# One DMA transpose for two units of dS in an attention backward loop

## The chip, the cores and the metric

The kernel runs on one core of a Trainium2 chip. The metric is the device time of one execution in microseconds, lower being better; every execution is timed on the device, and the median of several is taken.

## What is computed

The reference is the forward and backward pass of one transformer block (batch 1, 2048 tokens, width 512): layer norm with modulation by a conditioning vector, attention with 32 heads of 16 channels, and a feed-forward layer with a squared ReLU. The kernel returns the block's output and nine gradients. The part that matters here is the backward pass of attention:

```python
qkv = (x @ wqkv).reshape(B, S, 3, H, Dh)              # H = 32, Dh = 16
scores = einsum('bhqd,bhkd->bhqk', q, k) * Dh ** -0.5
p = softmax(scores, axis=-1)
o = einsum('bhqk,bhkd->bhqd', p, v)
...
_out, _vjp = jax.vjp(_f, A_x, A_wqkv, A_wo, B_w1, B_b1, B_w2, B_b2, c, w_mod)
_grads = _vjp(grad_out)
```

For every head it needs dS = p * (dP - delta), where dP = dO V^T, and from it dK = dS^T Q and dQ = dS K. The products for dK and dV contract over queries, and dS as it is computed (queries on the partitions) serves them directly. The product for dQ contracts over keys, so dS is needed a second time with keys on the partitions. That second form is made by a DMA transpose.

## The kernel before

The forward pass, the feed-forward backward pass and the gradients of the weights stand before and after the loop in question. The backward attention loop (lines 748 to 909) runs over **units**. A unit is one group of four heads (`hg`, 8 of them), one chunk of 512 keys (`kc`, 4), and one tile of 128 queries; the queries are counted as four tiles (`qi`) in each of four chunks (`qc`). There are 8 x 4 x 4 x 4 = 512 units, and four units that differ only in `qi` form a **block**; there are 128 blocks. Each unit is worked on in two half-units (`j`, two heads each).

For each unit:

- `score` (L791): TensorE multiplies Q and K for one head into PSUM (`psS_u`, or `psS_x`, which shares a bank with `dqacc`), and ScalarE takes the exponential into `E_u`.
- `dp_pair` (L807): TensorE makes dP for two heads in `psD_u` (two buffers), and VectorE multiplies it with `E_u` into `dS_u` (128 queries x 4 heads x 512 keys, bf16, 512 KB). The row maximum and delta are subtracted inside the matmuls, through extra rows of the operands.
- `transpose_unit` (L819): SyncE issues one DMA transpose of the unit's `dS_u` into one quarter of `dsT`, the block's tile.
- `k_quad` and `v_quad` (L825, L834): two units later TensorE accumulates dK from `dS_u` and dV from `E_u` in `accVK`.
- `dq_quad` (L850): in the last two half-units of the *next* block, TensorE multiplies the keys with the block's four transposed tiles into `dqacc`; ScalarE scales the result into `dQacc` or `dqtmp`, and GpSimd adds it up.

The order of the instructions on TensorE, ScalarE, VectorE and SyncE is the order in which this loop writes them (`manual_schedule`, L888); each engine runs its own in that order, and semaphores make it wait for the others. A half-unit issues its two scores, the dP pair of the half-unit before it, the transpose (if a unit was just completed), a k or v quad of two units earlier, and, at `sub` 6 and 7, the dq quads:

```python
                b = j // 8 - 1
                if sub >= 6 and 0 <= b < NU // 4:
                    for kt in (2 * (sub - 6), 2 * (sub - 6) + 1):
                        dq_quad(b, kt)
```

So between a block's last transpose (issued at j = 8b + 8) and its first dq quad (j = 8b + 14) lie six half-units of other work. `E_u` and `dS_u` have four buffers each (pool `ework`), `dsT` has two. Loads for the next group of heads are issued by ScalarE (`load`, L776) at planned half-units; the SyncE queue carries the transposes and, in the last group, four loads of gradients (`load_grads`, L742). After the loop another scheduler orders the remaining instructions.

Of the kernel before, what the change touches and what calls it, by code (L numbers as in the profile page):

```python
# [17 lines left out]
BF = dt.bfloat16  # L18
F32 = dt.float32

P = 128
# [13 lines left out]
def kernel(  # L35
# [21 lines left out]
    SP = nc.sync  # L57
# [221 lines left out]
    with ExitStack() as ph:  # L279
        wk = ph.enter_context(tc.tile_pool(name="phC", bufs=2))  # L280
        ework = ph.enter_context(tc.tile_pool(name="phCe", bufs=4))
# [364 lines left out]
        with ExitStack() as ph2:  # L646
# [3 lines left out]
            with tc.manual_schedule(engines={PE.engine, ACT.engine}):  # L650
                for u in range(NF + 6):
# [18 lines left out]
                    if pend and pend[0][0] <= u and not open_group[0] and not stepped:  # L670
                        _, f, args = pend.pop(0)
# [26 lines left out]
        with ExitStack() as ph2:  # L698
            pools["mm"] = ph2.enter_context(tc.tile_pool(name="psM2", bufs=8, space=bass.MemoryType.PSUM))
            while dense:  # L700
                for _ in dense.pop(0):
                    clock[0] += 1
                    if pend and not open_group[0] and pend[0][0] + 2 <= clock[0]:
                        _, f, args = pend.pop(0)
# [43 lines left out]
    with ExitStack() as ph:  # L748
        ework = ph.enter_context(tc.tile_pool(name="phIe", bufs=4))
# [7 lines left out]
        hst, bst, dqt, cur = {}, {}, {}, {}  # L757
# [12 lines left out]
        def at(j, f, *args):  # L770
            todo.setdefault(j, []).append((f, args))
# [19 lines left out]
        def score(u, hq, shared):  # L791
            hg, kc, qc, qi = units[u]
            st = hst[hg]
            qt = qc * 4 + qi
            if hq == 0:
                bst[u] = (ework.tile([P, 4, 512], BF, name="E_u", tag="E_u"),
                          ework.tile([P, 4, 512], BF, name="dS_u", tag="dS_u"))
            r = 32 * hq
            if shared:
                psS = psx.tile([P, 512], F32, name="psS_x", tag="px")  # L800
            else:
                psS = pss.tile([P, 512], F32, name="psS_u", tag="ps")
            PE.matmul(psS[:], st["q"][r:r + 32, qt * P:(qt + 1) * P], st["k"][r:r + 32, kc * 512:kc * 512 + 512],  # L803
                      start=True, stop=True, tile_position=(r, 0))
            ACT.activation(bst[u][0][:, hq, :], psS[:], AF.Exp, scale=SCALE)  # L805

        def dp_pair(u, pair):  # L807
            hg, kc, qc, qi = units[u]
            st = hst[hg]
            qt = qc * 4 + qi  # L810
            E_u, dS_u = bst[u]
            psD = psd.tile([P, 2, 512], F32, name="psD_u", tag="pd")
            for hi in range(2):
                r = 32 * (2 * pair + hi)
                PE.matmul(psD[:, hi, :], st["do"][r:r + 32, qt * P:(qt + 1) * P], st["v"][r:r + 32, kc * 512:kc * 512 + 512],  # L815
                          start=True, stop=True, tile_position=(r, 0))
            DVE.tensor_tensor(dS_u[:, 2 * pair:2 * pair + 2, :], psD[:], E_u[:, 2 * pair:2 * pair + 2, :], ALU.mult)  # L817

        def transpose_unit(u):  # L819
            hg, kc, qc, qi = units[u]  # L820
            if qi == 0:
                dqt[u // 4] = tpool.tile([P, 4, 16, P], BF, name="dsT", tag="dsT")
            SP.dma_start(out=dqt[u // 4][:, qi], in_=bst[u][1].rearrange("p h k -> p (h k)"), transpose=True)

        def k_quad(u):  # L825
            hg, kc, qc, qi = units[u]
# [7 lines left out]
        def v_quad(u):  # L834
            hg, kc, qc, qi = units[u]
            qt = qc * 4 + qi
            E_u, dS_u = bst.pop(u)
            acc = cur["vk"]
            for hq in range(4):
                PE.matmul(acc[32 * hq:32 * hq + DH, :], dOs_tok[:, qt, (hg * 4 + hq) * DH:(hg * 4 + hq + 1) * DH], E_u[:, hq, :],  # L840
                          start=False, stop=(qt == TT - 1), tile_position=(0, 32 * hq), skip_group_check=True)
            if qt == TT - 1:
                ACT.activation(hst[hg]["vk"][:, kc * 512:(kc + 1) * 512], acc[:], AF.Identity)  # L843
                if kc == QC - 1:
                    if hg >= HG - 2:
                        xs[hg, "vk"] = hst[hg]["vk"]
                    else:
                        at(cur["j"] + 4, load, dVKtP[hg], hst[hg]["vk"][:])
# [39 lines left out]
        with tc.manual_schedule(engines={PE.engine, ACT.engine, DVE.engine, SP.engine}):  # L888
            for j in range(2 * NU + 10):
                u, pair, sub = j // 2, j % 2, j % 8  # L890
                cur["j"] = j
                if j < 2 * NU:
                    if pair == 0 and units[u][1:] == (0, 2, 0) and units[u][0] + 1 < HG:
                        load_head(units[u][0] + 1)
                    for hi in range(2):
                        score(u, 2 * pair + hi, sub < 6 and (2 * sub + hi) % 3 == 2)
                if 1 <= j <= 2 * NU:
                    dp_pair((j - 1) // 2, (j - 1) % 2)
                    if (j - 1) % 2 == 1:
                        transpose_unit((j - 1) // 2)  # L900
                if 2 <= u < NU + 2:
                    (k_quad if pair == 0 else v_quad)(u - 2)
# [4 lines that stand above are left out]
                for f, args in todo.pop(j, ()):  # L907
                    f(*args)
            assert not todo
# [234 lines left out]
```

## Time and profile before

| | before |
|---|---|
| device time, median of 3 runs | 3060.49 us (3059.92 to 3061.36) |
| the profiled execution's own time | 3064.67 us |
| its span (first to last instruction) | 3062.8 us |
| the loop: first to last dS multiplication on VectorE | 1436.8 to 2872.4 us of the span |
| busy over the span: TensorE / ScalarE / VectorE / GpSimd | 81% / 71% / 58% / 17% |
| mean granted TensorE clock | 0.806 |
| DMA transposes of dS | 512, of 512 KB each |

The profile is one execution of the kernel. Its page gives busy shares of each engine, the span in 40 slices, the chain of work that ended last, and the costliest groups of instructions with the idle time before them and what ended it. PE is TensorE, PEld its weight loads, DVE VectorE, ACT ScalarE, POOL GpSimd, SP SyncE; a "q" behind the name (SPq) is the engine's sequencer, which issues DMAs. L823 is line 823 of the kernel. The busy time of SPq on a DMA is the time of issuing; the data move later, and a DMA piece in the chain runs from the issue to the landing.

### The profile page before, as it was taken

To read this page: it belongs to the slowest core of one execution; us is meant where nothing else is said; L and a number is where in the kernel's file an instruction comes from. 1 tells how busy PE (TensorE), PEld (TensorE's weight loads), DVE (VectorE), ACT (ScalarE), POOL (GpSimd) and SP (SyncE) were. 2 spreads that over 40 slices of the span, in tenths; PEclk is the share of its full clock that TensorE was granted. 3 is DMA by queue.
4 is the path that set the end of the run, shared out by engine and by line. 5 is a ranking of instruction groups with operands and counts; after the bars stand their busy time and mean duration, and the time that the engine had idled before them with its cause. 6 is when DMAs were issued, how large, how long until landed. Compare 5 with 4: busy or idle time off the path is not lost.

```text
span 3062.8 us, 46283 instructions
## 1 busy us (share of the span) xinstructions
PE 2481.7 (81%) x17006; PEld 720.8 (24%) x17006; DVE 1786.0 (58%) x2165; ACT 2181.0 (71%) x3415; POOL 519.5 (17%) x487
## 2 busy tenths in 40 slices
PE   6789888688867885565888888989888988888878
PEld 2111122222212221221222222222222222222323
DVE  6000134333513351446888878878887888878783
ACT  4699989698958894201777877878777877877521
POOL 2110012220332033313010110101011010101151
PEclk9555579878976997687888888878887798878889
DMA  9750142633394439596999999999999999999931
GB/s 258 189 134 18 30 74 82 150 92 81 81 162 65 95 79 151 103 165 189 205 200 208 199 202 199 197 206 202 208 197 201 201 198 205 204 204 204 212 107 52
DMA packets 1403811, 475.54 MB, mean 155 GB/s; under 512 B 1321456, under 2 KB 1372660, under 8 KB 1403456
## 3 DMA queue, kind: packets, MB, share of 16 engines
q1 hardware_dynamic: 1384624, 431.18, 73.8%
q0 software_dynamic: 12384, 25.17, 5.0%
q10 hardware_dynamic: 6576, 16.23, 1.6%
q8 instruction: 134, 2.20, 0.3%
q14 instruction: 93, 0.76, 0.1%
HBM read 74.86 MB, written 70.54 MB: 47 GB/s over the span
## 4 chain that ended last, share of the span: by engine, by line
PE 24%; DMA 19%; ACT 5%; DVE 5%; issue 3%; POOL 1%; SPq 1%; ACTq 0%; DVEq 0%; POOLq 0%
DMA dsT<-dS_u 16%; PE psS_u L803 7%; PE dqacc L858 5%; ACT E_u L805 5%; PE accVK L840 3%; PE accVK L831 3%; PE psS_x L803 2%; DVE dS_u L817 2%; DMA dwp<-dw_st 2%; PE pwq L1060 1%; PE psD_u L815 1%; SPq L954 0%; DMA out_dram<-dwm 0%; ACT vkb L843 0%; PE pm L496 0%
## 5 line engine op out<-in xcount | busy, mean ns | idle before, releaser
L817 DVE TENSOR_TENSOR dS_u<-psD_u,E_u 128x1024 bf16<-128x1024 f32 x1024 | 1190.4, 1218 | 250.0 <-PE psD_u L815 155.3
L573 ACT ACTIVATE ET<-psST 128x1024 bf16<-128x1024 f32 x1024 | 952.1, 1224 | 169.8 <-PE psST L571 168.8
L805 ACT ACTIVATE E_u<-psS_u 128x512 bf16<-128x512 f32 x1536 | 866.1, 632 | 272.0 <-PE psD_u L815 258.7
L805 ACT ACTIVATE E_u<-psS_x 128x512 bf16<-128x512 f32 x512 | 331.8, 648 | 18.0 <-PE psD_u L815 12.7
L858 PE MATMUL dqacc<-dsT,KS_tok 128*32 128x512 bf16 x2048 | 214.4, 506 | 140.8 <-DMA dsT<-dS_u 116.8
L803 PE MATMUL psS_u<-ik_10939,iq_10941 32*128 32x512 bf16 x768 | 260.5, 436 | 8.9 <-DVE prows L717 3.5
L803 PE MATMUL psS_u<-ik_11983,iq_11985 32*128 32x512 bf16 x768 | 264.5, 444 | 2.8
L587 PE MATMUL oacc<-ET,vaug 128*32 128x512 bf16 x2048 | 254.9, 488 | 1.3 <-DVE ostage L591 1.3
L815 PE MATMUL psD_u<-iv_11984,ido_11986 32*128 32x512 bf16 x1024 | 231.6, 446 | 13.7 <-DVE dS_u L817 11.8
L815 PE MATMUL psD_u<-iv_10940,ido_10942 32*128 32x512 bf16 x1024 | 225.1, 433 | 16.0 <-DVE dS_u L817 12.8
L873 POOL TENSOR_TENSOR dQacc<-dQacc,dqtmp 128x512 f32<-128x512 f32 x64 | 81.2, 1268 | 916.7 <-ACT dqtmp L868 916.7
L571 PE MATMUL psST<-qt_sb_107,kt_sb_105 32*128 32x512 bf16 x1024 | 201.1, 479 | 41.5 <-ACT ET L573 14.4
L840 PE MATMUL accVK<-E_u,dOs_tok 128*16 128x512 bf16 x2048 | 229.9, 439 | 0.0
L571 PE MATMUL psST<-qt_sb_108,kt_sb_106 32*128 32x512 bf16 x1024 | 196.4, 482 | 27.2 <-ACT ET L573 14.3
L342 DVE COPY dwp<-pm 128x512 f32<-128x512 f32 (+1 forms) x102 | 67.3, 660 | 240.5 <-DMA dw_st<-dwp 163.3
L591 DVE COPY ostage<-oacc 128x512 f32<-128x512 f32 x32 | 22.0, 686 | 266.2 <-PE oacc L587 266.2
L335 PE MATMUL pm<-tk,h_c 128*128 128x512 bf16 (+1 forms) x256 | 73.5, 421 | 89.7 <-DVE dwp L342 74.0
L831 PE MATMUL accVK<-dS_u,qz_11977 128*32 128x512 bf16 x1024 | 116.2, 442 | 7.6 <-ACT vkb L843 6.8
L831 PE MATMUL accVK<-dS_u,qz_11976 128*32 128x512 bf16 x1024 | 111.9, 427 | 10.0 <-ACT vkb L843 7.1
L803 PE MATMUL psS_x<-ik_11983,iq_11985 32*128 32x512 bf16 x256 | 108.5, 424 | 0.2
L803 PE MATMUL psS_x<-ik_10939,iq_10941 32*128 32x512 bf16 x256 | 105.6, 412 | 0.4 <-ACT E_u L805 0.2
L858 PEld LDWEIGHTS <-KS_tok 128*32 128x32 bf16 x2048 | 52.4, 106 | 202.2 <-issue 153.4
(747 smaller groups left out, 2558.8 us busy)
## 6 DMA issues: line engine op xcount, KB each, us to landing
dw_st<-dwp POOLq DMA_DIRECT2D x90, 256.0 KB, 4.2
dsT<-dS_u SPq DMA_TRANSPOSE x512
dwp<-dw_st SPq DMA_DIRECT2D x30, 256.0 KB
wA<-in_B_w_dram SPq DMA_DIRECT2D x4, 1792.0 KB
wB<-in_B_w_dram SPq DMA_DIRECT2D x4, 1792.0 KB
qkT_st<-qkT SPq DMA_DIRECT2D x4, 1024.0 KB
kt_sb_105<-qkT_st SPq DMA_DIRECT2D x64, 64.0 KB
kt_sb_106<-qkT_st SPq DMA_DIRECT2D x64, 64.0 KB
```

The lines of the kernel that those rows point to most:

```text
L335: PE.matmul(acc[:, 0:w], ops[ti][0], ops[ti][1], start=(ti == 0), stop=(ti == 3))
L571: PE.matmul(ps[:, hi, :], kt_sb[r:r + 32, kt * P:(kt + 1) * P], qt_sb[r:r + 32, :], start=True, stop=True, tile_position=(r, 0))
L573: ACT.activation(ET[:, 2 * pair:2 * pair + 2, :], ps[:], AF.Exp, scale=SCALE)
L587: PE.matmul(oacc[32 * hq:32 * hq + 32, :], lhsT, ET[:, hq, :], start=(kt == 0), stop=(kt == TT - 1), tile_position=(0, 32 * hq), skip_grou ...
L803: PE.matmul(psS[:], st["q"][r:r + 32, qt * P:(qt + 1) * P], st["k"][r:r + 32, kc * 512:kc * 512 + 512], start=True, stop=True, tile_positi ...
L805: ACT.activation(bst[u][0][:, hq, :], psS[:], AF.Exp, scale=SCALE)
L815: PE.matmul(psD[:, hi, :], st["do"][r:r + 32, qt * P:(qt + 1) * P], st["v"][r:r + 32, kc * 512:kc * 512 + 512], start=True, stop=True, til ...
L817: DVE.tensor_tensor(dS_u[:, 2 * pair:2 * pair + 2, :], psD[:], E_u[:, 2 * pair:2 * pair + 2, :], ALU.mult)
L831: PE.matmul(cur["vk"][32 * hq:32 * hq + 32, :], hst[hg]["qz"][:, qt, hq, :], bst[u][1][:, hq, :], start=(qt == 0), stop=False, tile_positi ...
L840: PE.matmul(acc[32 * hq:32 * hq + DH, :], dOs_tok[:, qt, (hg * 4 + hq) * DH:(hg * 4 + hq + 1) * DH], E_u[:, hq, :], start=False, stop=(qt ...
L858: PE.matmul(acc[32 * hq:32 * hq + 32, :], KS_tok[:, kc * 4 + kt, h * DH:h * DH + 32], tT[:, :, hq * 4 + kt, :], start=(kt == 0), stop=(kt ...
L873: POOL.tensor_tensor(dst2, dst, tmp[:], ALU.add)
```

## The change

The tile `dS_u` now holds two neighbouring units (128 x 2 x 4 x 512, 1 MB) and has three buffers instead of four of half the size. One DMA transpose is issued after the odd unit of each pair, and writes two quarters of `dsT`. There are 256 transposes of 1 MB in place of 512 of 512 KB. The order of all other instructions in the loop is the same. The k and v quads, the dq quads and `E_u` are unchanged.

```diff
             if hq == 0:
-                bst[u] = (ework.tile([P, 4, 512], BF, name="E_u", tag="E_u"),
-                          ework.tile([P, 4, 512], BF, name="dS_u", tag="dS_u"))
+                if u % 2 == 0:
+                    cur["ds"] = ework.tile([P, 2, 4, 512], BF, name="dS_u", tag="dS_u", bufs=3)
+                bst[u] = (ework.tile([P, 4, 512], BF, name="E_u", tag="E_u"), cur["ds"][:, u % 2], cur["ds"])
...
-            E_u, dS_u = bst[u]
+            E_u, dS_u, _ = bst[u]
...
             if qi == 0:
                 dqt[u // 4] = tpool.tile([P, 4, 16, P], BF, name="dsT", tag="dsT")
-            SP.dma_start(out=dqt[u // 4][:, qi], in_=bst[u][1].rearrange("p h k -> p (h k)"), transpose=True)
+            if qi % 2 == 1:
+                SP.dma_start(out=dqt[u // 4][:, qi - 1:qi + 1].rearrange("p t b q -> p (t b) q"),
+                             in_=bst[u][2].rearrange("p t h k -> p (t h k)"), transpose=True)
...
-            E_u, dS_u = bst.pop(u)
+            E_u = bst.pop(u)[0]
```

## The prediction

> **What bounds the kernel now.** I read the page's slices first, then its chain, then the backward loop alone (1437 to 2884 us of the span, 128 blocks of four units). The loop is where the DMA engines are full:
>
> ```profile
> PE   6789888688867885565888888989888988888878
> DMA  9750142633394439596999999999999999999931
> DMA dsT<-dS_u 16%; PE psS_u L803 7%; PE dqacc L858 5%; ACT E_u L805 5%; PE accVK L840 3%; PE accVK L831 3%; PE psS_x L803 2%; DVE dS_u L817 2%; DMA dwp<-dw_st 2%; PE pwq L1060 1%; PE psD_u L815 1%; SPq L954 0%; DMA out_dram<-dwm 0%; ACT vkb L843 0%; PE pm L496 0%
> ...
> L858 PE MATMUL dqacc<-dsT,KS_tok 128*32 128x512 bf16 x2048 | 214.4, 506 | 140.8 <-DMA dsT<-dS_u 116.8
> ```
>
> The largest item of the chain is the transpose, and the one long stall of PE in the loop is dq_quad waiting for it. The windows view (start and end, us, busy us of PE, PEld, DVE, ACT, POOL, granted clock, DMA share, GB/s) and the timeline of SP say the same of throughput:
>
> ```profile
> 1480.00:2870.00 1390.00, 1211.20 (x9959) 332.27 (x9957) 1158.32 (x997) 1092.15 (x2150) 135.81 (x100) 0.84 1.16 202
> ```
>
> ```profile
> 1998.29 102.85 SPq L823 DMA_TRANSPOSE dsT<-dS_u  x37
> ```
>
> The tile view of dsT gives counts and ns, shortest/median/longest, for the matmuls that read it and the transposes that write it:
>
> ```profile
> L858 PE MATMUL dqacc<-dsT,KS_tok x2048: 376/582/634, 1464.4 to 2883.6; 128*32 128x512 bf16 x187
> L823 SPq DMA_TRANSPOSE dsT<-dS_u x512: 1663/2538/11587, 1442.4 to 2877.8; - x171
> ```
>
> No compute engine is full (PE 87%, DVE 83%), SP issues without a pause, one transpose each 102.85/37 = 2.78 us. The wait table's 986.5 us of "SPq L823 <- DVE" is not a real wait: only 48 of 512 issues begin within 0.2 us of their dS being ready; the others began late because SP and the DMA engines were behind. So transfers queue, and the loop runs at their pace. But the chain inside one block shows a second bound, close behind (start us, us, what):
>
> ```profile
> 1994.28 7.33 DMA dsT<-dS_u
> 2001.61 0.14 issue
> 2001.74 1.04 PE dqacc L858 x8
> ...
> 2006.58 0.11 DVE dS_u L817
> 2006.69 6.80 DMA dsT<-dS_u
> 2013.49 0.25 issue
> 2013.74 0.59 PE dqacc L858
> ```
>
> It is a loop: the fourth unit's transpose lands, PE leaves its wait in dq_quad, and only then computes the scores and dP that stand behind it in program order; 5.08 us later the next block's fourth dS is ready (2001.61 to 2006.69), and its transpose takes 6.80 us more to land. A block cannot be shorter than **L_dma** (fourth dS ready to dq_quad released) plus **L_comp** (released to next fourth dS ready). Taken from the records of instructions and semaphores over 125 blocks, L_dma is 6.76 us on average, L_comp 4.40 us; the fourth dS's of first and last block, 127 intervals apart, give 11.21 us a block.
>
> **What the Trainium skill says.** "DMA: Bandwidth & Descriptors", Rules for kernel authors, asks for 1 MiB or more per DMA for maximum bandwidth; that speaks for the change. Its section on the anatomy of one DMA puts a fixed cost of about 2.0 us on a (software-issued) DMA, mostly completion latency; this trace shows that the latency overlaps in a full queue, since transposes follow at 2.78 us while one alone needs 4.7 us from ready to landed. "Perfetto Trace Analysis", DMA Optimizations, says the reverse: splitting "may allow some to start sooner". "TensorE: Matmul & The Clock Gate", Part 1, says that PE falls to half clock after idleness; the trace agrees, with dqacc matmuls of 376 ns at best and 582 ns at the median, and a mean granted clock of 0.84 in the loop.
>
> **The change, part by part.**
>
> 1. *256 transposes less.* Aligning the trace's 256-byte packets (2048 a transpose, 1,048,576 in all) at the first packet of undisturbed transposes, the rate is 85 to 87 per 0.1 us, with a dip to 58 lasting some 0.4 us where one DMA follows another. 2048 packets at 86 are 2.38 us; the undisturbed start-to-start median is 2.49. So a boundary costs about 0.11 us, and 256 fewer save at most 256 x 0.11 = 28 us of transfer. SP itself is relieved of 256 issues; it has nothing else to do here, so nothing.
>
> 2. *Even units wait for odd ones.* The transpose of units 4b and 4b+2 is issued one unit (2.8 us) later. Before, three units of the next block (4b+4 to 4b+6) were ready when PE stalled in block b's dq_quad, and filled the DMA engines for 3 x 2.49 = 7.5 us. Now unit 4b+6 waits for 4b+7, whose scores and dP stand behind that stall. Only the first pair, 2 x 2.49 - 0.11 = 4.87 us, is there to move. From the last packet of one second pair, the next second pair's first packet needs 0.63 (packet to landing) + 0.13 (hop to PE) + 4.75 (L_comp) + 1.24 (issue to first packet) = 6.75 us. The DMA engines then idle 6.75 - 4.87 = 1.9 us a block: the cover is gone.
>
> 3. *The whole second pair lies on the loop's path.* An undisturbed 512 KB transpose that found the queue empty took 4.70 us from ready to landed (median of nine, 4.43 to 5.22). No 1 MB transpose is in the trace. I add 2048 packets at 85 per 0.1 us, **2.40 us**, because the rate stays level within a transpose once past the dip; 4.70 + 2.40 = 7.10. Bounds: below, 1.15 us: in bursts after a stall the packets reach 113 per 0.1 us, so all 4096 take 3.62 us instead of the isolated 2.5 + 2.4 (the page's figure for transposes, section Latency and other measured facts, 261 GB/s, makes 4.0 us of 1 MB, an estimate in between); above, 2.79 us, the mean with all disturbances.
>
> 4. *Disturbances that fall on it.* 131 instruction-fetch packets in the loop each go with a transpose 0.77 us longer than the undisturbed (3.29 against 2.52), and those beside ACT's loads are 0.17 us longer, 27 us in all. Per block 1.02 x 0.77 + 0.21 = 1.0 us; the share 7.1/12.5 meets the second pair: 0.57 us. The rest hits the first pair, where the idle 1.9 us hides it. L_dma = 7.10 + 0.57 + 0.13 = **7.80 us**.
>
> 5. *L_comp.* It is 3.85 us with PE at full clock and 4.92 at half. The stall now grows to about 2 us in every block; after stalls over 1.8 us it was 4.5 to 4.93 in all 21 cases. I take **4.75**; bounds 4.2 and 4.92. Behind the waiting dq_quad on PE stand two more dq quads, four scores and four dP matmuls; ACT's exponentials and DVE's dS wait for these. ACT's own head loads slide along with it.
>
> 6. *Buffers.* dS_u goes from four units to three pairs. The first write of a pair needs the transpose three pairs back: ready to landed 7.7 us, and that write comes four units (12.5 us) after that dS was ready. Margin 4.8 us; without it DVE would wait and the block lengthen by the shortfall. DVE's present 30.6 us of waits for dsT may go; no gain, since L_dma and L_comp don't hold them. dsT stays double; its block's quads are over four half-units before it is rewritten. E_u is unchanged. The four gradient loads on SP pass at most one transpose; after the loop the scheduler orders a few loads and DVE instructions anew: zero, bounds -10 and +10 us.
>
> Sum: 7.80 + 4.75 = 12.55 us a block, against 11.21: 1.34 x 128 = **+172 us**. The profiled execution (3064.67 us, span 3062.8) would become 3237; the median of the runs is 4.2 lower, so 3060.49 + 172 = 3232 us. DVE (8 x 1.14 = 9.1 us a block) and PE have room in it.
>
> **Rivals.**
>
> - *Half-clock everywhere and queues behind the first pair* (0.10): L_dma from the median of all 48 empty-queue starts, disturbed ones too, 5.38 + 2.79 + 0.13 = 8.3, with L_comp 4.92: 13.2 us, +255 us, 3315. For it: stalls this long kept PE cold; against: part of the disturbance is counted twice.
> - *Faster, throughput decides* (0.08): the page's 1 MB rule holds, and packets flow at the burst rate of 113. Then L_dma = 1.49 (to first packet) + 3.62 + 0.63 + 0.13 + 0.57 = 6.4, and with the present L_comp of 4.40 a block takes 10.8 us: -47 us, 3013. It decides once the added half costs under 2.40 - 1.34 = 1.06 us. Against it: bursts appear only after a stall[...]; an undisturbed stream stays at 86.
> - *Gain and loss cancel* (0.03): L_comp stays near 3.9 because PE stays warm, and disturbances miss the second pair: 7.23 + 3.95 = 11.2 us, 3060.
> - *It doesn't do what it says*: a 1 MB transpose could have been cut in two again. The built program holds 256 transposes of 128x32x128 in place of 512 of 128x16x128, so this gets no chance.
>
> **How the numbers follow.** Forecast case 0.79, its own range 12.0 to 13.0 us a block, 3160 to 3290. A difference of 0.2%, 6 us, is about what a measurement of this kernel can tell from none. Downwards the range reaches to the page's 4.0 us for 1 MB with L_comp 4.2: 1.49 + 4.0 + 0.63 + 0.13 + 0.57 + 4.2 = 11.0 to 11.6 with 4.75; I take the upper end, +50, 3110. Upwards to 13.0, 3295. Left out: the fast and equal cases and half of the slowest. Faster 0.08, same 0.03, slower 0.89.
>
> **What would show it.** Right: PE's wait of dqacc on DMA dsT grows from 116.8 us to some 250; nearly every block's chain alternates a DMA piece of 7 to 8.5 us with 4.5 to 5 us of compute; the windows view shows the DMA share in the loop falling from 1.16 to about 1.05 and GB/s from 202 to about 180; SP shows gaps before every second transpose; a transpose alone moves its 4096 packets in about 4.9 us. Wrong: SP still without a pause, blocks near 11 us, or packets faster than 90 per 0.1 us within the 1 MB. If the stall grows but L_comp stays at 3.9, step 5 is mis-sized; if the loss sits on DVE waiting for dS_u, step 6 is.

## The result, and the profile after

The changed kernel is slower: 3249.1 us (median of four runs, 3239.27 to 3257.81) against 3060.2 us, a ratio of **1.0616**, with a 95% interval of 1.0584 to 1.0648. The profiled execution has a span of 3237.5 us against 3062.8. From the first dS multiplication to the end of the last the loop takes 1620 us instead of 1437 (+183); what stands ahead of it is 15 us shorter, what follows 6 us longer. This execution is the shortest of the four (3239.27 us), so its difference, 175 us, is smaller than the 189 us between the medians. One run of a later kernel, after_defer3, was slow at a low granted clock (3090.18 us at 0.661, its others at 0.796 to 0.812) and stands in no figure below.

First the page: slices of PE and DMA, the chain, and the row of dq_quad's matmuls. Behind its bar stand the busy us, the mean ns of one, and the idle time before it with what ended it.

```profile
PE   6789888678678854567787788787777888788778
DMA  9740143533663395879999999999999999999931
DMA dsT<-dS_u 31%; PE dqacc L861 7%; PE psS_u L804 4%; PE accVK L843 3%; DMA dwp<-dw_st 2%; PE accVK L834 1%; PE pwq L1063 1%; PE psS_x L804 1%; ACT E_u L806 1%; PE pdh L1029 1%; DVE dS_u L818 0%; DVE dwr L338 0%; DVE dx1J L1054 0%; DMA out_dram<-dwm 0%; PE pdc L978 0%
...
L861 PE MATMUL dqacc<-dsT,KS_tok 128*32 128x512 bf16 x2048 | 254.8, 592 | 305.1 <-DMA dsT<-dS_u 305.1
```

The transposes' part of the chain has doubled, from 16% to 31%, and dq_quad's wait on them went from 116.8 to 305.1 us. The slices still show a 9 for DMA nearly everywhere: a slice of 81 us is far too coarse for pauses of 2 us, and packets overlap. The windows view, the tile view of dsT and SyncE's timeline (start, duration, count) show them:

```profile
1480.00:3040.00 1560.00, 1248.46 (x9912) 327.74 (x9909) 1153.42 (x992) 1089.08 (x2136) 135.77 (x100) 0.78 0.97 179
```

```profile
L861 PE MATMUL dqacc<-dsT,KS_tok x2048: 376/634/635, 1450.1 to 3051.8; 128*32 128x512 bf16 x187
L825 SPq DMA_TRANSPOSE dsT<-dS_u x256: 4750/4888/13287, 1428.1 to 3042.7; - x128
...
  PE dqacc L861: 305.1, 128
```

```profile
2105.22 9.81 SPq L825 DMA_TRANSPOSE dsT<-dS_u  x2
...
2117.97 5.07 SPq L825 DMA_TRANSPOSE dsT<-dS_u  x1
```

DMA share and rate fell from 1.16 and 202 GB/s to 0.97 and 179. Every one of the 128 blocks now waits in dq_quad, and the median matmul there takes 634 ns against 582 before. The trace knows two granted clocks, full and half: a dqacc matmul takes 379 ns at the median under the full one and 634 under the half one, and 1724 of the 2048 now start under the half one, against 1028 before. SyncE issues two 1 MB transposes back to back (2105.22 + 9.81 = 2115.03) and then has nothing to issue for 2.94 us. The chain of the same block, in order of time (start us, us, what):

```profile
2105.22 7.66 DMA dsT<-dS_u
2112.88 0.14 issue
2113.02 1.05 PE dqacc L861 x8
2114.06 0.54 PE psS_u L804 x2
...
2115.14 0.85 PE dqacc L861 x8
2115.99 0.54 PE psS_u L804
...
2117.83 0.14 PE accVK L843
2117.97 7.13 DMA dsT<-dS_u
```

Landing, release, 5.09 us of compute (2112.88 to 2117.97), next transpose: the cycle of the prediction, now with no queue to hide it.

The quantities below are averages over the loop's blocks, taken from the start and end times of instructions, packets and semaphore updates in the traces. "SyncE idle" is the time from the end of one issue to the start of the next; about 0.1 us before each transpose is the pause between two issues that have all they need.

| kernel | us a block | L_dma | L_comp | SyncE idle a block | issuing a block |
|---|---|---|---|---|---|
| before | 11.22 | 6.76 | 4.40 | 0.51 | 10.73 |
| after | 12.64 | 7.85 | 4.76 | 2.44 | 10.22 |

L_dma and L_comp follow one another without a gap, so their sum is a block's length in any kernel, whatever bounds it. What tells the bound is who waits: here SyncE stands idle 2.4 us a block, and PE waits for the landing in every block. Of the growth, L_dma has 1.09 us and L_comp, computed at the half clock more often, 0.36.

### The profile page after: what moved, and what is told of

Read it like the earlier page. It is cut to its first block, busy times and chain, and to the rows that moved or that the text cites. A ratio compares the mean times of both kernels' runs of the same rounds, so it can differ in the third digit from the quotient of the medians.

```text
span 3237.5 us, 45347 instructions
## 1 busy us (share of the span) xinstructions
PE 2501.0 (77%) x16937; PEld 717.8 (22%) x17006; DVE 1787.4 (55%) x2165; ACT 2184.3 (67%) x3415; POOL 513.9 (16%) x487
## 4 chain that ended last, share of the span: by engine, by line
DMA 33%; PE 20%; DVE 3%; issue 2%; ACT 1%; SPq 1%; POOL 1%; ACTq 0%; DVEq 0%; POOLq 0%
DMA dsT<-dS_u 31%; PE dqacc L861 7%; PE psS_u L804 4%; PE accVK L843 3%; DMA dwp<-dw_st 2%; PE accVK L834 1%; PE pwq L1063 1%; PE psS_x L804 1%; ACT E_u L806 1%; PE pdh L1029 1%; DVE dS_u L818 0%; DVE dwr L338 0%; DVE dx1J L1054 0%; DMA out_dram<-dwm 0%; PE pdc L978 0%
## 5 line engine op out<-in xcount | busy, mean ns | idle before, releaser
L804 PE MATMUL psS_u<-ik,iq 32*128 32x512 bf16 x1536 | 535.3, 467 | 7.5 <-ACT E_u L806 2.1
L861 PE MATMUL dqacc<-dsT,KS_tok 128*32 128x512 bf16 x2048 | 254.8, 592 | 305.1 <-DMA dsT<-dS_u 305.1
L816 PE MATMUL psD_u<-iv,ido 32*128 32x512 bf16 x2048 | 479.0, 462 | 1.2
L571 PE MATMUL psST<-qt_sb,kt_sb 32*128 32x512 bf16 x2048 | 395.0, 476 | 69.1 <-ACT ET L573 28.6
L834 PE MATMUL accVK<-dS_u,qz 128*32 128x512 bf16 x2048 | 233.5, 445 | 21.5 <-ACT vkb L846 16.1
L804 PE MATMUL psS_x<-ik,iq 32*128 32x512 bf16 x512 | 222.5, 435 | 0.8
L804 PEld LDWEIGHTS <-iq 32*128 32x128 bf16 x2048 | 100.8, 94 | 416.4 <-issue 415.9
L571 PEld LDWEIGHTS <-kt_sb 32*128 32x128 bf16 x2048 | 81.9, 94 | 402.3 <-issue 392.0
L816 PEld LDWEIGHTS <-ido 32*128 32x128 bf16 x2048 | 119.1, 94 | 167.3 <-issue 140.4
L876 POOL TENSOR_TENSOR dQst<-dQacc,dqtmp 128x512 bf16<-128x512 f32 x32 | 40.6, 1268 | 342.2 <-ACT dqtmp L871 342.2
L834 PEld LDWEIGHTS <-qz 128*32 128x32 bf16 x2048 | 56.6, 95 | 171.5 <-issue 166.1
```

The lines of the kernel that those rows point to most:

```text
L571: PE.matmul(ps[:, hi, :], kt_sb[r:r + 32, kt * P:(kt + 1) * P], qt_sb[r:r + 32, :], start=True, stop=True, tile_position=(r, 0))
L834: PE.matmul(cur["vk"][32 * hq:32 * hq + 32, :], hst[hg]["qz"][:, qt, hq, :], bst[u][1][:, hq, :], start=(qt == 0), stop=False, tile_positi ...
L861: PE.matmul(acc[32 * hq:32 * hq + 32, :], KS_tok[:, kc * 4 + kt, h * DH:h * DH + 32], tT[:, :, hq * 4 + kt, :], start=(kt == 0), stop=(kt ...
L876: POOL.tensor_tensor(dst2, dst, tmp[:], ALU.add)
```

## The experiments

All ratios are against the kernel before on the same chip, with their 95% intervals; its median was 3056.6 to 3066.4 us there. The runs set three explanations apart: the path of the prediction (path theory), the size of a 1 MB DMA as such (size theory), and the three pair buffers of dS_u (buffer theory). A fourth, PE's half clock, is met further down.

**Buffers alone (pairtile_single).** The changed kernel's tiles, with one transpose a unit:

```diff
-            if qi % 2 == 1:
-                SP.dma_start(out=dqt[u // 4][:, qi - 1:qi + 1] ...)
+            SP.dma_start(out=dqt[u // 4][:, qi], in_=bst[u][1].rearrange("p h k -> p (h k)"), transpose=True)
```

> dS_u keeps the changed kernel's pair tiles with three buffers, but every unit has its own 512 KB transpose, issued when the unit is ready, as in the kernel before. Path theory (a block lasts from the fourth dS over its transpose's landing, dq_quad's release and the compute behind it to the next fourth dS, unless the DMA engines need longer): all of the loss goes, 3060 us, within 6. Size theory (1 MB transposes move their bytes more slowly): 3060 as well. Buffer theory (three pair buffers hold VectorE up): the loss stays, about 3249.

Measured: 3057.74 us, ratio 1.0003 (0.9992 to 1.0014), 11.24 us a block. The buffers cost nothing.

**A delay that was none (late_single).**

```diff
             if qi % 2 == 1:
+                for v in (u - 1, u):
+                    SP.dma_start(out=dqt[u // 4][:, units[v][3]], in_=bst[v][1]..., transpose=True)
```

> Pair tiles; two 512 KB transposes, both issued after the odd unit: the delay of the change without its size. Path theory: the fourth dS still has two transposes to wait for, L_dma about 7.9 us and L_comp 4.7, so 3250 to 3265 us with 256 boundaries more than the changed kernel. Size theory: close to before, 3060 to 3080.

Measured: 3057.04 us, ratio 0.9996 (0.9985 to 1.0007). The path theory's number failed, but the trace shows that the edit did not do what it was meant to. SyncE's queue holds nothing between the two transposes, and each waits only for the dS that it reads. In one pair the even unit's dS was ready at 1940.74 us, its transpose was issued at 1941.71, and the odd dS followed only at 1942.99. Moving the two lines in the program moved nothing in time, so this run says no more than pairtile_single.

**A real delay (odd_first).** As late_single, but with the odd unit's transpose ahead of the even one's, which makes the even one queue behind it:

```diff
-                for v in (u - 1, u):
+                for v in (u, u - 1):
```

> Pair tiles, 512 KB transposes, but in SyncE's queue the odd unit's comes first, so that the even unit's really is held back until the odd dS is ready (in late_single each still started on its own dS, as SyncE waits only for what a transpose reads). Path theory: two transposes lie behind the fourth dS; L_dma 7.9 to 8.1 us, L_comp 4.7, SyncE idle 2 us a block before each second pair: 3245 to 3275 us. Size theory (1 MB in one DMA is what costs): 3060 to 3090.

Measured: 3234.76 us, ratio **1.0549** (1.0522 to 1.0575), 12.55 us a block. The tile view of dsT in odd_first:

```profile
L861 PE MATMUL dqacc<-dsT,KS_tok x2048: 376/634/634, 1460.0 to 3048.9; 128*32 128x512 bf16 x187
L826 SPq DMA_TRANSPOSE dsT<-dS_u x512: 1678/2465/11567, 1437.5 to 3043.6; - x171
...
  DMA dsT<-dS_u: 253.6, 106
```

There is no 1 MB DMA here, only 512 of 512 KB, and nearly all of the loss is back, with the same cycle: L_dma 7.79 us, L_comp 4.71 us, SyncE idle 1.95 us before the second pair. The median is 10 us under the expected range. So the delay of the even unit is the cause; to the size it leaves at most the last 0.09 us of the 1.42 that a block grew by.

**Which pair (first_pair, second_pair).** Both have 128 transposes of 1 MB and 256 of 512 KB; only the place differs.

```diff
-            if qi % 2 == 1:
+            if qi == 1:            # second_pair: qi == 3
                 SP.dma_start(... two units ...)
+            elif qi >= 2:          # second_pair: qi < 2
+                SP.dma_start(... one unit ...)
```

> Pair tiles; the first two units of a block share one 1 MB transpose, the third and fourth have their own 512 KB. Path theory: behind the fourth dS lies 512 KB again, and 1 MB plus 512 KB (5.0 + 2.5 us) cover the 6.75 us until it; no loss, 3040 to 3075 us. Size theory: half of the 1 MB transposes, half of the loss, about 3155.

> Pair tiles; the first two units of a block have their own 512 KB, the third and fourth share one of 1 MB: as many transposes of each size as with the first pair merged. Path theory: the whole loss, 3235 to 3260 us, since the 1 MB lies behind the fourth dS. Size theory: half of the loss, about 3155.

Measured: first_pair 3093.64 us, ratio 1.0119 (1.0098 to 1.0139); second_pair 3253.68 us, ratio **1.0645** (1.0627 to 1.0663). second_pair has all of the loss with half of the merging: SyncE idle 2.27 us before the 1 MB, L_dma 7.89 us. first_pair is where the path theory failed by more than its band: +37 us where -20 to +15 were expected. L_dma is nearly as before (7.01 us), but SyncE is idle 0.82 us before the merged pair (over 0.3 us in 65 of 127 blocks), against 0.18 us before the first unit in the kernel before. The fourth transpose is issued, the first unit of the next block is already there (ready 0.9 us before SyncE was free, at the median of those 65), and the 1 MB must wait for the second unit: it starts 0.03 us after that one is ready. A merge starves the DMA engines wherever its last part is late, not only in front of dq_quad.

**The middle pair (middle_pair).** To test that, units two and three were merged (dS_u in two pair and three single buffers):

```diff
-            if qi % 2 == 1:
+            if qi == 2:
                 SP.dma_start(... units 1 and 2 of the block ...)
+            elif qi != 1:
+                SP.dma_start(... one unit ...)
```

> The second and third unit of a block share a 1 MB transpose; the first and the fourth have their own 512 KB (dS_u in two pair and three single buffers). With the first pair merged, SyncE idled 0.83 us a block since the second unit's dS was not ready when the queue had run dry; here the first unit's transpose fills that time, and the fourth keeps 512 KB behind it. Path and throughput: SyncE idle before the pair 0.3 us, 0.25 us saved by the merge: 3045 to 3070 us. If any merged pair costs what the first one did: 3090 to 3100.

Measured: 3086.7 us, ratio 1.0065 (1.0044 to 1.0085), above the expected band. The direction is right and the size is not: SyncE is idle 0.61 us before the pair (over 0.3 us in 58 of 128 blocks), twice the expected 0.3 and less than first_pair's 0.82. The first unit's 512 KB bridge only part of the time.

**Smaller still (half_units).** 1024 transposes of 256 KB, each issued with its half-unit:

```diff
...
-                    if (j - 1) % 2 == 1:
-                        transpose_unit((j - 1) // 2)
+                    transpose_unit((j - 1) // 2, (j - 1) % 2)
```

> The other direction: one 256 KB transpose for each half-unit, 1024 in all, issued when its half is ready. Path theory: less lies behind the fourth dS, but throughput decides, with four boundaries more a block: at the 0.11 us of the prediction 11.65 us a block, 3115 us; at the 0.25 us by which SyncE's time a block fell per merged pair, 12.2 us, 3185 us. If the landing of the fourth dS alone decided, its 1.2 us less would make it faster, about 2920.

Measured: 3156.75 us, ratio 1.0303 (1.0275 to 1.0331), 11.98 us a block, 0.76 more than before for four more transposes, 0.19 us each. This is between the two values expected. The piece that lies behind the fourth dS got shorter (L_dma 6.16 us against 6.76), and the kernel got slower, so landing was not the only bound of the kernel before: its issue and transfer time was full. Whether SyncE's issuing or the DMA engines set the 0.19 us is not told apart here.

**The landing taken off the path (after_defer, before_defer).** Every dq_quad eight half-units later:

```diff
-            for j in range(2 * NU + 10):
+            for j in range(2 * NU + 18):
...
-                b = j // 8 - 1
+                b = j // 8 - 2
```

> The changed kernel with every dq_quad eight half-units later (a block's dq quads at the end of the block after next). Path theory: the cycle over the landing is cut, the wait of dq_quad on dsT vanishes, and SyncE's issue without pauses decides: 10.2 + 0.3 us a block, 2965 to 3010 us, faster than both kernels. Clock theory (the loss is PE at half clock, whatever it waits for) and size theory: over 3150 still.

> The kernel before with the same delay of dq_quad. Path and throughput: SyncE and the DMA engines were already issuing without pause, 10.7 + 0.5 us a block; PE's waits on dsT vanish but move to VectorE's wait for dS_u: 3030 to 3062 us. If the wait of dq_quad had been the bound by itself (compute needs some 9.4 us a block): 2850 to 2950.

Measured: after_defer 3100.38 us, ratio 1.012 (1.0094 to 1.0147); before_defer 3386.73 us, ratio 1.1054 (1.1027 to 1.1082). Both were expected lower. Four fifths of the loss went away in the first, at nearly the same granted clock in the loop (0.79 against 0.78 in the changed kernel): the half clock alone is not what costs. But a new wait came in both: dsT has two buffers, and with the quads a block later the first transpose of a block must wait for the quads of two blocks before. In before_defer it starts 0.05 us after the last of them has ended. SyncE is idle 3.40 us a block before it in before_defer, 0.94 us in after_defer; that a pair asks for its buffer one unit later would explain the difference, but no run tests it.

**With a third dsT buffer (before_defer3, after_defer3, defer3_single).**

```diff
-        tpool = ph.enter_context(tc.tile_pool(name="phIt", bufs=2))
+        tpool = ph.enter_context(tc.tile_pool(name="phIt", bufs=3))
```

In the changed kernel this needs room: `E_u` with three buffers, `dqtmp` with one, `r_inv` in a pool of the forward pass. defer3_single is after_defer3 with 512 KB transposes.

> The kernel before with dq_quad eight half-units later and a third dsT buffer, since with two the first transpose of a block had to wait for the dq quads of two blocks before (SyncE idle 3.4 us there). Path and throughput: the landing is off the path and no buffer is in the way; SyncE's issue time decides, 10.7 + 0.5 us a block as before: 3045 to 3070 us, PE's wait of dqacc on dsT near nothing, VectorE's wait for dS_u in its place. If the landing of the fourth dS had been a bound of its own beside throughput: 2950 to 3020.

> The changed kernel with dq_quad eight half-units later and a third dsT buffer; to make room E_u has three buffers, dqtmp one, and r_inv lies in a pool of the forward pass. Path and throughput: SyncE's 10.4 us of 1 MB issues and 0.3 us of gaps a block, 2990 to 3020 us, faster than before by what the fewer issues save (0.25 us for each merged pair). If 1 MB issues save nothing against two of 512 KB: 3045 to 3070. If three pair buffers of dS_u hold VectorE up, SyncE idles and it stays near the 3100 us of two dsT buffers.

> after_defer3 in everything (late dq_quad, third dsT buffer, pair tiles, three E_u buffers, one dqtmp, r_inv moved), but each unit has its own 512 KB transpose. If the merge is what made after_defer3 faster: 3050 to 3070 us, 11.2 us a block as in before_defer3, SyncE without idle time. If the buffers or the moved tile did it: near 3032 us.

Measured: before_defer3 3058.6 us, ratio 0.9975 (0.9964 to 0.9987); **after_defer3 3031.17 us, ratio 0.9882** (0.9865 to 0.9899); defer3_single 3049.48 us, ratio 0.9975 (0.9965 to 0.9985), just under its expected range. after_defer3 beats both kernels, but by less than the expected 2990 to 3020 us. That range took a merged pair to save the 0.25 us by which the issuing of a pair fell in the table above. Yet issuing falls as much, to 10.13 us a block, in before_defer with its 512 KB transposes: it falls where SyncE has stood idle, and was no saving of the merge. The windows view and the tile view of dsT in after_defer3:

```profile
1480.00:2860.00 1380.00, 1231.33 (x10138) 350.67 (x10142) 1164.94 (x1019) 1104.71 (x2160) 142.16 (x106) 0.85 1.18 209
```

```profile
L861 PE MATMUL dqacc<-dsT,KS_tok x2048: 376/379/634, 1467.5 to 2840.2; 128*32 128x512 bf16 x187
L825 SPq DMA_TRANSPOSE dsT<-dS_u x256: 4773/5079/13288, 1440.5 to 2831.2; - x128
...
  DVE dS_u L818: 105.7, 62
```

The tile view of dsT in before_defer3:

```profile
L858 PE MATMUL dqacc<-dsT,KS_tok x2048: 378/461/634, 1468.7 to 2881.3; 128*32 128x512 bf16 x187
L823 SPq DMA_TRANSPOSE dsT<-dS_u x512: 1705/2580/11575, 1437.5 to 2874.4; - x171
...
  DVE dS_u L817: 132.1, 103
...
  PE dqacc L858: 5.1, 1
```

In after_defer3 PE is not among the waiting any more, the median dq_quad matmul runs at full clock (379 ns), the DMA engines move 209 GB/s, more than in the kernel before, and what is left is VectorE's wait for a free dS_u: throughput alone. There the merge pays. after_defer3 takes 10.87 us a block, defer3_single 11.13; two transposes fewer a block save 0.27 us, **0.13 us each**. The ratio of the two ratios, 0.9882/0.9975, makes that 0.9% of the time. before_defer3 has the same block time as the kernel before (11.23 us against 11.22), and PE waits for dsT once (5.1 us) where it waited 116.8 us: in the kernel before, throughput was the bound, and the cycle over the landing had only just room beside it.

## Why the prediction was right

The prediction was +172 us to 3232, the measurement +189 to 3249.1. Its forecast case is the one that happened: the cover of the queue is gone, and the second pair's landing and the compute behind it set a block. Its terms can be read one by one.

- *Step 1, fewer boundaries.* That the boundaries' saving could not be collected here is confirmed, and within the 1 MB the packets kept their rate of 85 per 0.1 us. The 0.11 us a boundary is near the 0.13 us that the merge saved in the deferred loop, but not for the reason given. There, 1 MB with no other traffic beside it takes 4.96 us as two transposes (defer3_single, median of 54) and 5.03 us as one (after_defer3, median of 42), from first packet to next first packet: nothing is saved. The gain lies where other traffic runs beside: 5.20 against 5.10 us with ScalarE's loads alone, 5.85 against 5.50 with instruction fetches alone. Why the larger transpose suffers less from them stays open.
- *Step 2, the starving DMA engines.* It expected 1.9 us a block of idle DMA engines; from the last packet of the first pair to the first of the second it is 2.1 us (over 0.3 us in 123 of 128 blocks). SyncE idles 2.3 us there, of which 0.1 is the ordinary pause.
- *Step 3, the second pair on the path.* The packets of a second pair take 5.13 us at the median, first to last, not 4.9: 0.2 us more. They start 1.21 us after the dS is ready, as the 1.24 said; the 1.49 of the isolated singles was too much here, so the two errors cancel. The 261 GB/s behind the lower end of its range stand in the Trainium skill, "DMA: Bandwidth & Descriptors", Latency and other measured facts, for a non-contiguous middle dimension, and 350 to 400 for the contiguous case; the rows here are contiguous, and 1 MB with no other traffic took 5.03 us, 208 GB/s.
- *Step 4, disturbances.* L_dma came to 7.85 us against 7.80. Readiness to landing is 7.73 us on average and 6.86 at the tenth percentile, so the disturbances weigh some 0.9 us, more than the 0.57, while the undisturbed base is lower than 7.10. The sum is right by cancelling, which is luck.
- *Step 5, L_comp.* 4.76 us against 4.75. The half clock came as expected: 634 ns for the median dqacc matmul. L_comp is 4.92 us in the 53 of 127 blocks that compute at half clock throughout, so the rival that took 4.92 for every block was too high.
- *Step 6, buffers.* VectorE's wait for dsT fell from 30.6 us to 3.9 in the whole span, and pairtile_single shows the buffers to be neutral.
- *The sum.* 12.64 us a block against 12.55. Over 127 intervals the growth is 181 us. The span of the profiled execution, 3237.5 us where 3237 was forecast, agrees better than the block does, and that is luck too: the stretch ahead of the loop, put at no change, was 15 us shorter in this trace. It lies between 1422 and 1437 us in the traces of all the kernels here, whose code does not differ there except for where `r_inv` lies in two of them.
- *The rivals.* Gain by throughput did not come, because the second half of the 1 MB would have had to cost under 1.06 us, and it cost 2.6 (5.13 less the 2.5 of a 512 KB transpose). The expected signs mostly fit: the wait of dqacc rose to 305 us rather than 250, GB/s to 179 as foreseen, the DMA share to 0.97 instead of 1.05.

What the prediction did not see is the other side of step 2. It counted what a merged pair leaves behind dq_quad, but not what it costs when the queue runs dry while the pair's own second unit is still being computed. In the change itself that wait is hidden behind the longer stall (SyncE is idle only 0.15 us before the first pair); first_pair and middle_pair brought it out.

## What to carry to other kernels

When a transfer feeds a consumer that stands ahead, in program order, of the work that produces the next transfer, follow the cycle from producer over landing and consumer back to producer, and count how many bytes lie behind the last producer; merging doubles them. First give the consumer slack (later quads and a buffer for each block in flight), and only then merge: the same merge cost 6.2% without the slack and gained 0.9% with it. Writing a DMA's issue later in the program delays nothing when its queue holds nothing in between, since the transfer waits only for its own data (late_single).

## What the runs showed of the hardware

- DMA transposes of 512 KB from SBUF to SBUF, one behind the other and undisturbed, take 2.49 us (210 GB/s), those of 1 MB 5.03 to 5.15, no less than two of the small ones. After a transpose that was held up, packets are seen at up to 113 per 0.1 us for about one transpose, then at 85 again.
- The larger transpose does not run faster inside. The 0.13 us a boundary that it saved in the deferred loop is an average over transposes with and without other traffic beside them. The shortest issue on SyncE was 1.23 us for 256 KB, 1.66 for 512 KB, 4.75 for 1 MB: the last is not twice the second but near the transfer itself.
- Fetching of instructions goes through the same DMA engines: some 130 packets of 8 or 16 KB in the loop of the kernel before. The transposes beside them were longer than the undisturbed ones, by 0.7 to 0.8 us on average. By the same comparison these and ScalarE's loads made up about 1 us of the 11.2 us of a block.
